# Output-weight mixing in a fused attention and maxout kernel: the same work planned at wider spacing, its stores later

## The chip, the core and the metric

The kernel runs on one NeuronCore of a Trainium2 chip. The engines are named as the profile names them: PE does the matrix products (PEld is its weight load), DVE, ACT and POOL do elementwise work, and SP issues all the DMAs of the stage that this document is about. The metric is the device time of one execution in microseconds; a smaller number is better. Before the change it is 638.62 us, the median of three runs (637.04 to 640.19).

## What is computed

Attention within chunks of 64 positions, then a layer that takes the maximum of three products, then an output layer:

```python
scores = scale * np.matmul(q_c, k_c.transpose(0, 1, 2, 4, 3))
attn = np.exp(scores - np.max(scores, axis=-1, keepdims=True))
attn = attn / (np.sum(attn, axis=-1, keepdims=True) + 1e-09)
x = np.matmul(attn, v_c)                       # as 4608 rows of 512
h = np.maximum(np.maximum(x @ w1, x @ w2), x @ w3)   # 768 columns
return h @ w_out                                     # 512 columns
```

Every fp32 operand of a large product is kept as a high and a low part, and one product is three PE instructions: low by high, high by low, high by high.

## The kernel before

The 36 tiles of 128 rows go in six pieces. Two groups of four tiles are multiplied plainly (`moe`). The other 28 tiles go in four units of 7, 8, 7 and 6 tiles (`unit`), which use a scheme with seven block products in the place of eight. The seven are taken in the order 1, 6, 5, 2, 7, 3, 4 (`ORDER`). For this scheme the weights must be mixed first: sums and differences of 256-wide blocks.

**The inner layers.** A unit runs nine "layers" (`hidden(n)`, two 128-column blocks of one of the three inner weights each). A layer is seven block products of six PE instructions, 42 in all, of 448 columns in the first unit (line 590). Its mixed weights lie in DRAM (`w0` to `w8`; rows print them as `w_1273` and so on). They come by two loads: line 515 fetches the first part, which products 1, 2 and 4 use, and line 519 the second part, for products 6, 5, 7 and 3. There are two buffers of each part (`ring`), so the load for layer n+2 is planned for the end of layer n and can only be issued when PE has finished with layer n. In the first unit `w_1273` belongs to the third layer, `w_1145` to the fourth, `w_874` to the fifth and `w_1017` to the sixth.

**What PE needs from the other engines.** The products of a layer share PSUM banks: products 2, 7 and 3 add onto the banks of 1, 6 and 5, so ACT must have copied those banks to `kept` (line 568) first. Before the first unit, the second group's output layer is multiplied (line 172 to 174, tiles `ao`, ACT copy and store at lines 329 and 330), and its last bank is wanted by the first layer's third product. Between products PE also does three short attention steps, which this document calls an attention insert: values (line 257), scores (line 222) and transpose (line 245) of the tiles of the next unit. ACT, DVE and POOL do their softmax.

**The mixing of the output weights.** `store_out(jp)` does it for three blocks, jp 0 to 2, during the first unit. Each block does on POOL two additions that put high and low part together (`f`, line 413) and four sums (`c`, line 427); on ACT the high part of the result (`sh`, line 432); on DVE the low part (`sl`, line 436); and on SP sixteen small stores to the DRAM tensor `wo`: eight "originals" of weights as they are (lines 448 and 450) and eight "mixed" ones (line 457, four of `sh` and four of `sl`). The tiles `f`, `c`, `sh` and `sl` have one buffer each, so the blocks follow one another. `wo` is first read near the end of the unit's inner layers (line 526).

**What sets the order.** The program's order on each engine is fixed when it is built. `plan(at, pe, fn)` puts a piece of work into a list by a planned time, and `passed` writes it down when the plan's clock, which advances by a nominal time per PE step, has reached it. So the numbers are no times on the chip: they only decide what stands before what on each engine. At run time every engine and the SP queue go strictly in that order, and each instruction waits for its inputs. The SP queue also counts its transfers on eight semaphores in turn, so an issue waits until the transfer eight places earlier has landed.

Of the kernel before, what the change touches and what calls it, by code (L numbers as in the profile page):

```python
# [62 lines left out]
def chunk_attn_maxout_kernel(  # L63
# [284 lines left out]
    minus, plus, most = ALU.subtract, ALU.add, ALU.max  # L348
# [56 lines left out]
    def store_out(jp):  # L405

        j, st = 2 * jp, {}

        def whole(c):
            def fn():  # L410
                if c == 0:
                    st["f"] = att.tile([P, 2, DO], F32, name="f", tag="qs", bufs=1)
                nc.gpsimd.tensor_tensor(out=st["f"][:, c], in0=woh[:, j + c].bitcast(F32), in1=wol[:, j + c].bitcast(F32),
                                        op=plus)
            return fn

        def part(k, c):
            return lambda: st["f"][:, c, k * 256:(k + 1) * 256]

        def sums(k):  # L420
            return lambda: st["c"][:, k]

        def sum_of(k, x, y, op, first=False):
            def fn():
                if first:
                    st["c"] = att.tile([P, 4, 256], F32, name="c", tag="rv", bufs=1)
                nc.gpsimd.tensor_tensor(out=st["c"][:, k], in0=x(), in1=y(), op=op)
            return fn

        def high():  # L430
            st["h"] = late["hold"].tile([P, 4, 256], F32R, name="sh", tag="k0", bufs=1)
            nc.scalar.copy(out=st["h"], in_=st["c"])

        def low():
            st["l"] = late["hold"].tile([P, 4, 256], F32R, name="sl", tag="k1", bufs=1)
            nc.vector.tensor_tensor(out=st["l"], in0=st["c"], in1=st["h"].bitcast(F32), op=minus)

        def to(first, step, many, m, h):
            w = outer_w["w"].rearrange("p (m i j h x) -> p m i j h x", m=2, i=7, j=3, h=2)
            return w[:, m, first:first + step * (many - 1) + 1:step, jp, h]  # L440

        def originals():
            if jp == 0:
                outer_w["w"] = dram.tile([P, 14 * 768], F32, name="wo")
            for h, src in enumerate((woh, wol)):
                for m in range(2):
                    cols = slice(m * P, (m + 1) * P)
                    nc.sync.dma_start(out=to(0, 3, 2, m, h), in_=src[:, j:j + 2, cols].bitcast(F32))
                    cols = slice(256 + m * P, 256 + (m + 1) * P)
                    nc.sync.dma_start(out=to(6, 1, 1, m, h), in_=src[:, j + 1:j + 2, cols].bitcast(F32))  # L450

        def mixed():
            for h, src in enumerate("hl"):
                for m in range(2):
                    cols = slice(m * P, (m + 1) * P)
                    for half in range(2):
                        nc.sync.dma_start(out=to(1 + 3 * half, 1, 2, m, h),
                                          in_=st[src][:, 2 * half:2 * half + 2, cols].bitcast(F32))

        a11, a12, a21, a22 = part(0, 0), part(0, 1), part(1, 0), part(1, 1)  # L460
        return [(0.0, whole(0)), (1.1, whole(1)), (1.5, originals), (2.2, sum_of(1, a21, a22, plus, True)),
                (2.9, sum_of(0, sums(1), a11, minus)), (3.6, sum_of(2, a11, a21, minus)),
                (4.3, sum_of(3, a12, sums(0), minus)), (5.6, high), (6.8, low), (8.4, mixed)]

    turns = [0, 0]

# [306 lines left out]
    def plan(at, pe, fn):  # L773
        heapq.heappush(due, (at, len(order), pe, fn))
        order.append(fn)
# [109 lines left out]
    def stores_out():  # L885
        for jp in range(3):
            for at, fn in store_out(jp):
                plan(now + 11.5 + 8.0 * jp + at, 0.0, fn)

    inner = 3 * JT * CT * STEP + UNITS[0] * TILE  # L890
    def span(u):
# [2 lines left out]
    def outer_span(u):  # L894
# [3 lines left out]
    parts += [("steps", lambda j=j, w=w: g["hidden"](j, w)) for j in range(JT) for w in range(3)]  # L898
    parts += [("do", change), ("do", lambda: operands(0, OPERANDS)), ("do", lambda: last_operands(0, 10.5)),
              ("do", stores_out),  # L900
              ("do", lambda: tiles(1, 4 * JT * STEP + span(0))), ("do", lambda: load(0, 0, 0.0, 1.0)), ("do", lambda: load(0, 1, 2.0, 3.0))]
    parts += [("steps", lambda: g["project"](0, 1)), ("steps", lambda: g["project"](2)), ("steps", lambda: g["project"](3))]
# [11 lines left out]
    now = -10.0  # L914
# [54 lines left out]
```

## Time and profile before

| | before |
|---|---|
| median of three runs | 638.62 us (637.04 to 640.19) |
| profiled execution, its own time | 638.54 us |
| its span, first to last instruction | 636.8 us |
| mean granted PE clock | 0.992 |
| busy share of PE / PEld / DVE / ACT / POOL | 97 / 84 / 70 / 44 / 46 % |

The profile is one execution. Times in rows are microseconds from the first instruction; the time outside the span is 1.7 us. The stage of the change lies between 175 and 235 us.

### The profile page before, as it was taken

The page shows a single profiled execution, that of the slowest core. Times are in us where ns is not written, and L with a number is a line of the kernel's source. Part 1 is how long each engine was busy: PE and PEld are TensorE (multiplying, and loading weights), DVE is VectorE, ACT ScalarE, POOL GpSimd, SP SyncE. Part 2 cuts the span into 40 slices and gives each one's busy share as a digit, 9 for nine tenths or more (in the row PEclk, how much of TensorE's full clock was granted, in tenths as well). Part 3 has the DMA queues.
Part 4 walks back from the last instruction along what each step waited for, and adds up shares of the span by engine and source line. Part 5 has one row for each costly group of instructions (what it writes and reads, how often), then busy time and mean ns, then how long its engine had stood idle before and what let it go on. Part 6 is the DMA issues. An engine that isn't in the chain of part 4 may idle for free.

```text
span 636.8 us, 12715 instructions
## 1 busy us (share of the span) xinstructions
PE 618.1 (97%) x5101; PEld 536.1 (84%) x5102; DVE 444.8 (70%) x676; ACT 277.3 (44%) x491; POOL 294.8 (46%) x243
## 2 busy tenths in 40 slices
PE   7899999999988799999999999999999999999997
PEld 3788878878877689899887888888999999999997
DVE  4889854788856566879648687895496668366761
ACT  4888633454533253535424342443342435332341
POOL 2423577765487333435524353472253437233441
PEclk9999999999989799999999999999999999999999
DMA  8978459576968976548946474578655659776675
GB/s 327 376 282 308 181 183 355 213 243 231 349 200 253 307 309 227 227 171 297 374 183 267 157 286 155 227 260 325 251 214 195 248 190 306 262 269 247 232 257 188
DMA packets 52042, 161.26 MB, mean 253 GB/s; under 512 B 5264, under 2 KB 21392, under 8 KB 46224
## 3 DMA queue, kind: packets, MB, share of 16 engines
q1 hardware_dynamic: 51984, 160.45, 70.3%
q8 instruction: 40, 0.66, 0.4%
q14 instruction: 18, 0.15, 0.1%
HBM read 128.97 MB, written 31.46 MB: 252 GB/s over the span
## 4 chain that ended last, share of the span: by engine, by line
PE 80%; DVE 9%; ACT 3%; DMA 3%; POOL 2%; issue 2%; SPq 0%; POOLq 0%; ACTq 0%; DVEq 0%
PE pm L590 61%; PE pm L172 4%; PE pm L173 4%; PE pm L174 4%; PE s L257 2%; DMA ring<-w 2%; PE tp L245 2%; PE s L222 2%; DVE e L232 1%; DVE s L383 1%; DVE sm L180 1%; DVE mx L227 1%; PE pm L735 1%; ACT e L236 1%; DMA w<-s 1%
## 5 line engine op out<-in xcount | busy, mean ns | idle before, releaser
L590 PE MATMUL pm<-X,ring 128*128 128x448 f32 (+2 forms) x1584 | 333.6, 368 | 9.5 <-DMA ring<-w 5.2
L590 PEld LDWEIGHTS pm<-X,ring 128*128 128x128 f32 x1584 | 293.0, 190 | 39.8 <-ACT kept L568 3.8
L568 ACT COPY kept<-pm 128x448 f32<-128x448 f32 (+2 forms) x132 | 69.7, 533 | 141.8 <-PE pm L590 118.1
L590 PE MATMUL pm<-Y,ring 128*128 128x448 f32 (+2 forms) x432 | 91.7, 364 | 0.0
L575 POOL TENSOR_TENSOR kept<-kept 128x448 f32<-128x448 f32 (+2 forms) x44 | 55.7, 1265 | 76.6 <-ACT kept L568 76.2
L590 PEld LDWEIGHTS pm<-Y,ring 128*128 128x128 f32 x432 | 79.4, 188 | 7.8 <-DVE Y L626 0.5
L601 DVE TENSOR_TENSOR most<-pm,most 128x448 f32<-128x448 f32 (+2 forms) x72 | 44.6, 620 | 46.3 <-PE pm L590 45.4
L172 PE MATMUL pm<-xh,wl 128*128 128x512 f32 (+1 forms) x156 | 60.8, 390 | 0.0
L173 PE MATMUL pm<-xl,wh 128*128 128x512 f32 (+1 forms) x156 | 58.4, 374 | 0.3 <-DVE xl L268 0.3
L174 PE MATMUL pm<-xh,wh 128*128 128x512 f32 (+1 forms) x156 | 58.4, 375 | 0.0
L189 POOL TENSOR_TENSOR e<-e,sm 128x512 f32<-128x512 f32 x26 | 27.9, 1074 | 62.4 <-DVE sm L186 56.7
L579 POOL TENSOR_TENSOR kept<-kept 128x448 f32<-128x448 f32 (+2 forms) x24 | 30.7, 1279 | 49.3 <-DVE kept L571 44.8
L571 DVE TENSOR_TENSOR kept<-pm,kept 128x448 f32<-128x448 f32 (+2 forms) x44 | 27.2, 618 | 35.5 <-PE pm L590 30.5
L626 DVE TENSOR_TENSOR Y<-most,Y 128x448 fp32r<-128x448 f32 (+2 forms) x60 | 48.9, 834 | 3.5 <-ACT Y L623 3.1
L623 ACT CAST Y<-most 128x448 fp32r<-128x448 f32 (+2 forms) x60 | 33.3, 568 | 24.0 <-DVE most L601 16.9
L227 DVE TENSOR_REDUCE mx<-s 128x8 f32<-128x512 f32 x36 | 24.6, 684 | 22.9 <-PE s L222 22.9
L232 DVE TENSOR_TENSOR e<-s,mx 128x512 f32<-128x512 f32 x36 | 24.8, 689 | 16.8 <-ACT stage L271 16.4
L236 ACT ACTIVATE e<-e 128x512 f32<-128x512 f32 x36 | 22.8, 632 | 30.8 <-DVE e L232 30.8
L172 PEld LDWEIGHTS pm<-xh,wl 128*128 128x128 f32 x156 | 29.4, 188 | 5.5
L174 PEld LDWEIGHTS pm<-xh,wh 128*128 128x128 f32 x156 | 29.4, 188 | 5.4
L250 ACT COPY xs<-tp 128x512 f32<-128x512 f32 x36 | 21.0, 583 | 29.7 <-PE tp L245 29.6
L173 PEld LDWEIGHTS pm<-xl,wh 128*128 128x128 f32 x156 | 29.4, 189 | 5.1 <-DVE xl L268 0.5
(98 smaller groups left out, 860.0 us busy)
## 6 DMA issues: line engine op xcount, KB each, us to landing
ring<-w SPq DMA_DIRECT2D x36, 1024.0 KB, 6.6
ring<-w SPq DMA_DIRECT2D x36, 768.0 KB, 4.5
ring<-wo SPq DMA_DIRECT2D x28, 768.0 KB, 5.4
buf<-in_qk SPq DMA_DIRECT2D x36, 512.0 KB, 6.6
buf<-in_vb SPq DMA_DIRECT2D x36, 256.0 KB, 5.9
w<-s SPq DMA_DIRECT2D x9, 1024.0 KB, 5.4
stage<-in_w SPq DMA_DIRECT2D x7, 512.0 KB, 4.9
out_t<-ao SPq DMA_DIRECT2D x16, 224.0 KB, 4.1
```

Of the source, the lines that this page charges most:

```text
L172: nc.tensor.matmul(out=o, lhsT=al, rhs=bh, start=first, stop=False)
L173: nc.tensor.matmul(out=o, lhsT=ah, rhs=bl, start=False, stop=False)
L174: nc.tensor.matmul(out=o, lhsT=ah, rhs=bh, start=False, stop=last)
L227: nc.vector.tensor_reduce(out=st["mx"].rearrange("p (g c) -> p c g", c=2), in_=st["s"], axis=AX.X, op=ALU.max)
L232: nc.vector.tensor_tensor(out=st["e"].rearrange("p g c k -> p c g k"), in0=st["s"], in1=most.unsqueeze(3).broadcast_to([P, 2, 4, 64]), op= ...
L568: return lambda: nc.scalar.copy(out=kept(k), in_=o[i])
L575: (0.95, lambda: nc.gpsimd.tensor_tensor(out=kept(2), in0=kept(2), in1=kept(0), op=plus))],
L579: (1.0, lambda: nc.gpsimd.tensor_tensor(out=c22(), in0=kept(3), in1=kept(1), op=plus))],
L590: nc.tensor.matmul(out=o[i], lhsT=a, rhs=b, start=new and k == 0, stop=last and k == 2, skip_group_check=i in banks_of_product)
L601: return lambda: nc.vector.tensor_tensor(out=M(k, c), in0=of(), in1=M(k, c), op=most)
L623: return lambda: nc.scalar.copy(out=y_room(i, jp)[:, 0, :half], in_=t[i]())
L626: return lambda: nc.vector.tensor_tensor(out=y_room(i, jp)[:, 1, :half], in0=t[i](), in1=y_room(i, jp)[:, 0, :half].bitcast(F32), op=minus)
```

## The change

Two tables of planned times change, nothing else. The steps of one block are spread from 8.4 to 17 planned us. The blocks begin at 16, 30 and 44 planned us after the output layer of the second group begins, where it was 11.5, 19.5 and 27.5. The work and the bytes are the same.

```diff
-        return [(0.0, whole(0)), (1.1, whole(1)), (1.5, originals), (2.2, sum_of(1, a21, a22, plus, True)),
-                (2.9, sum_of(0, sums(1), a11, minus)), (3.6, sum_of(2, a11, a21, minus)),
-                (4.3, sum_of(3, a12, sums(0), minus)), (5.6, high), (6.8, low), (8.4, mixed)]
+        return [(0.0, whole(0)), (2.1, whole(1)), (3.5, originals), (4.2, sum_of(1, a21, a22, plus, True)),
+                (5.9, sum_of(0, sums(1), a11, minus)), (7.6, sum_of(2, a11, a21, minus)),
+                (9.3, sum_of(3, a12, sums(0), minus)), (12.0, high), (13.4, low), (17.0, mixed)]
...
-                plan(now + 11.5 + 8.0 * jp + at, 0.0, fn)
+                plan(now + 16.0 + 14.0 * jp + at, 0.0, fn)
```

On ACT, around the end of the second group's output layer and the first layer of the unit, there stands before (`sh` is the mixing, `kept` and `most` are the layer's copies, `xs`, `stage` and `e` an attention insert's):

```order
166 L236 ACTIVATE e<-e 128x512
167 L432 CAST sh<-c 128x1024
168 L329 COPY ao<-pm 128x512
169 L568 COPY kept<-pm 128x448 x3
170 L577 COPY most<-pm 128x448
171 L432 CAST sh<-c 128x1024
172 L250 COPY xs<-tp 128x512
173 L271 COPY stage<-s 128x2x4x64
174 L236 ACTIVATE e<-e 128x512
175 L568 COPY kept<-pm 128x448 x3
176 L432 CAST sh<-c 128x1024
```

and now:

```order
166 L236 ACTIVATE e<-e 128x512
167 L329 COPY ao<-pm 128x512
168 L568 COPY kept<-pm 128x448 x3
169 L577 COPY most<-pm 128x448
170 L250 COPY xs<-tp 128x512
171 L271 COPY stage<-s 128x2x4x64
172 L236 ACTIVATE e<-e 128x512
173 L432 CAST sh<-c 128x1024
174 L568 COPY kept<-pm 128x448 x3
...
178 L568 COPY kept<-pm 128x448 x3
179 L432 CAST sh<-c 128x1024
```

The first `sh` moved from before the `ao` copy to before the second layer's `kept` copies, and the second one from the end of the first layer to the third layer.

On SP, from the second block's last originals to the loads for the fifth layer, there stands before:

```order
128 L450 DMA wo<-woh 128x128
129 L210 DMA buf<-in_qk 128x1024
130 L457 DMA wo<-sh 128x2x128 x4
131 L457 DMA wo<-sl 128x2x128 x4
132 L515 DMA ring<-w_1273 128x1536
133 L519 DMA ring<-w_1273 128x2048
...
144 L457 DMA wo<-sh 128x2x128 x4
145 L457 DMA wo<-sl 128x2x128 x4
146 L515 DMA ring<-w_1145 128x1536
147 L519 DMA ring<-w_1145 128x2048
...
150 L515 DMA ring<-w_874 128x1536
151 L519 DMA ring<-w_874 128x2048
```

and now, from the load for the third layer to the second part of that for the fifth:

```order
119 L515 DMA ring<-w_1273 128x1536
120 L519 DMA ring<-w_1273 128x2048
...
123 L457 DMA wo<-sh 128x2x128 x4
124 L457 DMA wo<-sl 128x2x128 x4
125 L448 DMA wo<-woh 128x2x128
...
132 L450 DMA wo<-wol 128x128
133 L515 DMA ring<-w_1145 128x1536
134 L519 DMA ring<-w_1145 128x2048
...
137 L515 DMA ring<-w_874 128x1536
138 L457 DMA wo<-sh 128x2x128 x4
139 L457 DMA wo<-sl 128x2x128 x4
140 L519 DMA ring<-w_874 128x2048
```

Before, all mixed stores of two blocks stood ahead of the third layer's load. Now none does; the first block's mixed stores and the second block's originals (16 issues) stand between the loads for the third and the fourth layer, and the second block's mixed stores between the two parts of the fifth layer's.

On PE the order of the instructions is the same as before.

## Rows read from the trace of the kernel before

**Rows 1.** The page: busy time by engine, and the costliest group.
```profile
PE 618.1 (97%) x5101; PEld 536.1 (84%) x5102; DVE 444.8 (70%) x676; ACT 277.3 (44%) x491; POOL 294.8 (46%) x243
...
L590 PE MATMUL pm<-X,ring 128*128 128x448 f32 (+2 forms) x1584 | 333.6, 368 | 9.5 <-DMA ring<-w 5.2
```

**Rows 2.** Timeline of PE: start, duration, line, operands, count, [idle before, releaser].
```profile
178.79 2.59 PE L590 MATMUL pm<-X,ring 128*128 128x448 f32 x12
183.72 6.74 PE L590 MATMUL pm<-X,ring 128*128 128x448 f32 x24 [2.34 <-ACT ao L329]
...
197.60 5.13 PE L590 MATMUL pm<-X,ring 128*128 128x448 f32 x24 [0.60 <-ACT kept L568]
...
205.38 1.47 PE L590 MATMUL pm<-X,ring 128*128 128x448 f32 x6 [0.97 <-DMA ring<-w]
209.82 9.74 PE L590 MATMUL pm<-X,ring 128*128 128x448 f32 x36 [2.98 <-DMA ring<-w]
220.79 1.45 PE L590 MATMUL pm<-X,ring 128*128 128x448 f32 x6 [1.23 <-DMA ring<-w]
...
228.88 6.50 PE L590 MATMUL pm<-X,ring 128*128 128x448 f32 x30 [1.25 <-ACT kept L568]
```

**Rows 3.** Chain of waits, undisturbed: attention insert, then 48 products (start, duration).
```profile
235.38 0.62 PE s L257 x32
...
237.06 9.73 PE pm L590 x48
```

**Rows 4.** Windows: length, busy us of PE, PEld, DVE, ACT, POOL; granted clock.
```profile
184.00:187.00 3.00, 3.00 (x9) 2.68 (x9) 0.73 (x3) 1.07 (x3) 2.10 (x2) 0.50 0.78 251
208.00:214.00 6.00, 4.17 (x11) 3.77 (x12) 2.19 (x5) 2.12 (x4) 0.95 (x1) 0.50 0.83 217
221.00:224.00 3.00, 3.00 (x76) 2.56 (x76) 1.62 (x3) 0.58 (x2) 1.49 (x1) 1.00 1.00 410
```

**Rows 5.** Timeline of ACT around the first and second `sh`.
```profile
182.13 1.05 ACT L432 CAST sh<-c 128x1024 fp32r<-128x1024 f32 x1 [0.15 <-POOL c L427]
183.09 0.58 ACT L329 COPY ao<-pm 128x512 f32<-128x512 f32 x1
...
192.45 1.05 ACT L432 CAST sh<-c 128x1024 fp32r<-128x1024 f32 x1 [3.90 <-POOL c L427]
...
197.03 1.38 ACT L568 COPY kept<-pm 128x448 f32<-128x448 f32 x3
```

**Rows 6.** Timeline of the SP queue: start of issue, duration, transfer.
```profile
197.63 2.40 SPq L457 DMA_DIRECT2D wo<-sl  x4
200.13 0.41 SPq L515 DMA_DIRECT2D ring<-w  x1
200.58 0.46 SPq L519 DMA_DIRECT2D ring<-w  x1
...
209.71 0.32 SPq L450 DMA_DIRECT2D wo<-wol  x1
...
215.57 0.41 SPq L515 DMA_DIRECT2D ring<-w  x1
```

**Rows 7.** Waits of the SP queue, 200 to 216: total us, times, longest.
```profile
SPq L450 <- DMA ring<-w: 4.0, 1, 4.0
```

**Rows 8.** Line 515, three loads issued 200 to 221, issue to landing.
```profile
DMA to landing us min/median/max: 5.1/5.1/7.3
```

**Rows 9.** Line 519, three loads issued 200 to 221, issue to landing.
```profile
DMA to landing us min/median/max: 7.1/9.1/10.6
```

**Rows 10.** Line 519, three loads issued 240 to 270, issue to landing.
```profile
DMA to landing us min/median/max: 6.3/6.5/6.5
```

**Rows 11.** Line 436 (`sl`): duration ns min/median/max; then timelines of DVE and POOL.
```profile
L436 DVE TENSOR_TENSOR sl<-c,sh x3: 1224/1226/2321, 183.2 to 203.8; 128x1024 fp32r<-128x1024 f32 x3
...
193.54 2.32 DVE L436 TENSOR_TENSOR sl<-c,sh 128x1024 fp32r<-128x1024 f32 x1 [1.23 <-ACT sh L432]
...
193.49 3.52 POOL L413 TENSOR_TENSOR f<-woh,wol 128x512 f32<-128x512 f32 x2
```

## Prediction

> **What bounds the kernel now.** I read the page first. PE is busy 97% of the span, and its largest group, the layers' products at line 590, has 9.5 us of idle time before it, most of it put down to DMA [rows 1]. Since PE is full elsewhere, only these idle stretches can be won back. The waits of PE by stretch put all of them into 180 to 229 us, the first four layers of the first unit; after 235 us PE waits for nothing. So whatever is won or lost here goes through to the end.
>
> PE's timeline names six stops [rows 2]: 2.34 us for the copy of `ao`, 0.60 for `kept`, 0.97 and 2.98 for the third layer's load, 1.23 for the fourth's, and 1.25 for `kept` again, 9.37 together. Two of them cost twice. Undisturbed, 48 products take 9.73 us, 0.203 each, and an attention insert 1.68 (235.38 to 237.06) [rows 3]. After the 2.34 stop 24 products take 6.74 instead of 4.87, and after the 2.98 stop 36 take 9.74 instead of 7.30: 1.8 and 2.4 us lost. The granted clock was 0.50 in these stretches, the lower of the two levels, and 1.00 after the 1.23 stop [rows 4]. Each stop also has a tail: 24 products at full clock after the 0.60 stop take 5.13, 0.25 above 4.87.
>
> The causes stand on ACT and SP. The mixing's first `sh` waited 0.15 us for POOL and ran 1.05 ahead of the `ao` copy [rows 5]. On SP the third layer's load was issued at 200.13, right after the second block's `sl` stores [rows 6]. PE had finished the first layer, and with it the buffer, near 193.3 (24 products to 190.4, an insert, six more) [rows 2, 3]. The load was 6.8 us late. The fourth layer's load, at 215.57, came right behind the third block's stores, 12.9 us after its buffer was free at 202.7 (197.60 + 5.13) [rows 2].
>
> **The change, part by part.** POOL, ACT, DVE and SP do the same instructions; only places move. I lay the new order along PE, with 1.22 us for six products and 1.68 for an insert.
>
> (a) *The `ao` copy.* Without `sh` ahead it starts 1.05 + 0.15 = 1.2 us earlier, and PE goes on at 182.5 after a stop of about 1.15. The nearest row is the 1.23 stop, after which the clock stayed at 1.00 [rows 2, 4], so the 1.8 us go too: gain 3.0. If the clock falls all the same, it is 1.2.
>
> (b) *`kept` in the second layer.* The 0.60 stop came when the second `sh` and the doubled `sl` (2.32) pushed the insert's work on ACT, and `kept` with it, to 197.03 [rows 5, 11]. Neither stands there now: gain 0.85 with its tail. But the first `sh` now stands right ahead of these copies, and the second right behind those of the third layer. POOL's fourth sum for the first `sh` follows an addition that waits for product 7 of the first layer (18 products after 182.5, 186.2); by an estimate it is done before 191, so `sh` runs 191 to 192 and the first `kept` is there by 192.5; product 2 needs it at 194. It costs nothing while that cover of 1.5 us holds; bounds are 0 and 0.6 a place by the row of before. I take 0.3 at each: -0.6.
>
> (c) *The third layer's load.* From 182.5: 24 products to 187.4, an insert to 189.1, six to 190.3. Now the load is issued there, at 190.4 and 190.9, with 16 transfers fewer ahead. It lands 6.5 (undisturbed) to 10.6 us after issue [rows 9, 10], 197.4 to 201.5; its second part is needed at 201.7 (18 + 24 products to 198.8, insert to 200.5, six more). So both stops go: 0.97 + 2.98 + 2.4 for the clock + 0.5 for two tails = 6.85.
>
> (d) *The fourth layer's load.* It has the first block's 8 mixed stores and the second block's 8 originals ahead of it. An issue waits for the transfer eight places earlier: before, line 450 waited 4.0 us for a load in this way, till 209.71 [rows 6, 7]. So the second `sl` store cannot go before the third layer's load has landed, near 198. Then 3 stores and 8 originals of some 0.52 us (2.40 for four with small waits [rows 6]) make 5.7, and the load is issued at 203.7 and 204.2; its buffer was free at 198.8, so it is still 5 us late. The third layer ends 42 products after 200.5, at 209.0; its first part lands 5.1 later at 208.8 [rows 8]. The second is needed six products and an insert on, at 211.9. By the landings 7.1 and 9.1 it comes at 211.3 to 213.3; the mean, 212.3, is 0.4 late. Bounds: on time, or with everything at 9.1 (landing third layer 200.0, issue 206.3) at 215.4, 3.5 late. The stop of 1.23 + 0.25 shrinks to 0.4: gain 1.1.
>
> (e) *`kept` in the fourth layer*, 1.25: the same ACT and DVE order, PE going on with it, so it stays [rows 2]. DVE has the second block's `sl` (1.22) a little earlier, in the third layer, which pushes the chain by 0 to 1.2; there is idle time on DVE ahead of the copies, so nearer 0: -0.2.
>
> (f) *The fifth layer's load.* This is new. Its first part is issued when the third layer ends, 209.1, but the second stands behind 8 mixed stores, and the eighth of these waits for the landing of the first part, 5.1 to 7.3 us on [rows 8]. I take 6.1, as two loads and the fourth layer's are nearly drained by then: 215.2, the second part goes at 215.7. With 6.5 (little is queued ahead) it lands at 222.2. PE needs it at: 211.9 + 0.4, 18 products, the stop (e), 18 more (220.7 without the 0.4), six of the fifth layer: 222.3. No slack: I take 0.3 for a stop, between 0 and 5.2 (7.3 and then 10.6: 227.5).
>
> (g) *The rest.* The third block's originals and mixed stores now go out until about 233, one layer ahead of what overwrites `woh` and `wol` (near 242) and 40 us ahead of the first read of `wo`. The sixth layer's load, behind eight originals whose last waits for the fifth's second part, goes at 224.5 and is needed at 231 to 234. I cost these at nothing; the cover is 3 to 10 us.
>
> **Sum**: 3.0 + 0.85 - 0.6 + 6.85 + 1.1 - 0.2 - 0.3 = 10.7. From the profiled 638.54 (span 636.8 and 1.7 outside) that gives **627.8**; the median of the runs, 638.62, is the same within 0.1.
>
> **The rivals.**
>
> *1. The loads stay late.* The moved stores now stand ahead of other loads. For it: in (d) 16 issues are still ahead, in (f) there is no slack. Against: the stores' stretch now has 14 planned us a block. With the second part of the fifth layer issued at 216.9 and 10.6 on the way, PE stops 5.2 us, with 2.4 for the clock and a tail 7.85: 635.3. With the fourth's at 215.4 instead it is 3.5 + 2.65, 633.5; the two don't add, since the later PE is, the less the other is late. The Trainium skill (DMA: Bandwidth & Descriptors, Queues, rings and completion order) says that each DMA engine takes the descriptors of a queue in order, so that a load drains behind the stores issued ahead of it; by that rule this rival is the case. The rows agree in part: 9.1 and 10.6 beside stores against 6.5 [rows 9, 10].
>
> *2. POOL gets in DVE's way.* `sl` took 2.32 beside POOL's `f` and 1.22 without [rows 11]. If the spread-out `f` (1.76 each) meets the short chain on DVE ahead of `kept` in (e), the stop grows by 1.3 to 2.5, where the clock fell: +3.7, 631.5. Against: by my layout `f` ends at 211.4 and the chain begins near 213.5. The Trainium skill (SBUF — State Buffer, Who interferes with whom) has the rule: a DVE instruction with two SBUF inputs and a POOL instruction that reads SBUF share a port, and the later blocks. The 2.32 agrees with it.
>
> *3. It does not do what it says at the first stop*: PE's wait for `ao` is really one for something else that came last. Then (a) is nothing: 630.8. Against: `ao` ends and PE starts within 0.1 us [rows 2, 5].
>
> *4. Slower.* The fifth layer's load waits twice in the queue: its first part takes 10.6 (landing 219.7, which holds the eighth store), its second part, issued at 220.2, 10.6 again: 230.8, 8.5 late, with clock and tail 11.15, which gives 638.7. It decides from a landing past 231 on; every us later is a us slower than before. For it: the waiting rule of [rows 7] is certain. Against: no first part took more than 7.3 here.
>
> **How the numbers follow.** Forecast (626 to 630) 0.62; rival 1 0.15; rival 2 0.10; rival 3 0.08; rival 4 0.05. A measurement of this kernel can tell about 0.5%, 3.2 us, so faster means below 635.4: all of the first, half of rival 1 and rivals 2 and 3, 0.87. Within 0.5%: the other half of rival 1 and half of rival 4, 0.10; slower 0.03. The range goes down to 626.0 (no costs in b, d, e and f and a little of the `ao` stop) and up to rival 1 at 635.4.
>
> **What would show it.** PE's timeline after: a stop of about 1.2 near 181.4 with the clock at 1.00 after it; none at the third layer; 0 to 0.5 in the fourth ahead of product 6; 1.3 for `kept`; at most 0.5 ahead of product 6 of the fifth. On SP the third layer's load near 190.4, the fourth's near 203.7, the two parts of the fifth's some 6.6 us apart. It is wrong if the granted clock shows 0.50 anywhere past 182, or if PE names `ring` for more than 2 us.

## The result, and the profile after

The changed kernel takes 632.76 us, the median of eight runs (630.71 to 635.71); the kernel before took 638.5 in eight runs on the same chip. The ratio is 0.9916 with a 95% interval of 0.989 to 0.9941: faster by 5.7 us, where 10.7 was forecast. The time lies inside the range (626.0 to 635.4), well above the 627.8 that the sum gave. Single runs of the changed kernel scatter over 5 us, those of before over 3. The profiled execution of after took 635.71 (span 633.9), the longest of its eight, and is only 2.8 under the profiled execution of before; a second profile of the same kernel, below, took 634.37.

PE's timeline after, its stops alone (columns as in [rows 2]):

```profile
181.89 5.13 PE L590 MATMUL pm<-X,ring 128*128 128x448 f32 x24 [0.91 <-ACT ao L329]
203.98 5.23 PE L590 MATMUL pm<-X,ring 128*128 128x448 f32 x24 [0.23 <-ACT kept L568]
212.24 1.45 PE L590 MATMUL pm<-X,ring 128*128 128x448 f32 x6 [3.04 <-DMA ring<-w]
220.34 5.28 PE L590 MATMUL pm<-X,ring 128*128 128x448 f32 x24 [1.31 <-ACT kept L568]
226.49 1.45 PE L590 MATMUL pm<-X,ring 128*128 128x448 f32 x6 [0.87 <-DMA ring<-w]
237.73 2.71 PE L590 MATMUL pm<-X,ring 128*128 128x448 f32 x12 [0.68 <-DMA ring<-w]
249.19 3.33 PE L590 MATMUL pm<-X,ring 128*128 128x448 f32 x15 [0.99 <-DMA ring<-w]
549.99 58.51 PE L590 MATMUL pm<-X,ring 128*128 128x384 f32 x336 [1.98 <-DMA ring<-w]
```

Of the six stops of [rows 2], both for the third layer's load are gone, and after the stop for `ao` 24 products take 5.13 and not 6.74. The stop for the fourth layer's load has grown from 1.23 to 3.04, and there are new ones at the fifth, sixth and seventh layer, which the sum had at 0.3, 0 and 0.

How far PE is ahead of the kernel before, at the same place of its order (differences of the starts in both timelines of PE):

| place | before | after | ahead by | since the row above | forecast |
|---|---|---|---|---|---|
| start of the first layer | 178.79 | 178.38 | 0.41 | | |
| insert in the first layer | 190.38 | 186.95 | 3.43 | +3.0 | (a) +3.0 |
| insert behind the second layer | 202.66 | 198.35 | 4.31 | +0.9 | (b) +0.85 - 0.3 |
| end of the third layer | 219.56 | 209.21 | 10.35 | +6.0 | (c) +6.85 - 0.3 |
| insert in the fourth layer | 222.17 | 213.62 | 8.55 | -1.8 | (d) +1.1 |
| insert in the fifth layer | 235.31 | 227.87 | 7.44 | -1.1 | (e), (f) -0.5 |
| insert in the sixth layer | 246.72 | 240.37 | 6.35 | -1.1 | (g) 0 |
| insert in the seventh layer | 257.52 | 252.46 | 5.06 | -1.3 | (g) 0 |
| end of the span | 636.8 | 633.9 | 2.9 | -2.2 | 0 |

So PE was 10 us ahead at the end of the third layer, as forecast, and gave half of it back within the next four, for loads that came late.

The SP queue after shows why (columns as in [rows 6]):

```profile
192.43 3.35 SPq L457 DMA_DIRECT2D wo<-sh  x4
195.87 5.08 SPq L457 DMA_DIRECT2D wo<-sl  x4
201.00 1.48 SPq L448 DMA_DIRECT2D wo<-woh  x1
...
206.42 0.37 SPq L515 DMA_DIRECT2D ring<-w  x1
...
209.24 0.33 SPq L515 DMA_DIRECT2D ring<-w  x1
209.66 2.83 SPq L457 DMA_DIRECT2D wo<-sh  x4
214.62 5.32 SPq L457 DMA_DIRECT2D wo<-sl  x4
219.99 0.68 SPq L519 DMA_DIRECT2D ring<-w  x1
```

The waits of that queue from 186 to 250 (total, times, longest) name what it waited for:

```profile
SPq L457 <- DMA ring<-w: 9.9, 5, 2.7
...
SPq L450 <- DMA ring<-w: 1.6, 1, 1.6
SPq L457 <- DMA buf<-in_qk: 1.3, 2, 0.9
```

The fourth layer's load goes at 206.4 (203.7 in the forecast). Of these 2.7 us, 1.4 are lost by the first original, at 201.0: the four `sl` stores waited 1.6 us for the third layer's load and then 0.3 and 0.9 for the two input loads behind it. The rest is lost in the eight originals, which take 5.4 us and not 4.2; the first issue alone took 1.48, and the profile names no wait for it.

The second part of the fifth's load goes at 220.0 (215.7 in the forecast). The last `sl` store ahead of it waited 2.7 us, till 219.58, for the landing of the load's own first part. From issue (209.24) to landing that part took:

```profile
DMA to landing us min/median/max: 10.3/10.3/10.3
```

At nearly the same moment, 219.95, landed the store that stands eight places ahead of the second part. The chain of waits (start, duration) goes by that store:

```profile
209.66 10.29 DMA wo<-sh
...
219.99 6.37 DMA ring<-w
...
228.18 9.41 DMA ring<-w
```

That store of 128 KB was issued behind the fourth layer's load, two input loads and the first part of the fifth's. From issue to landing, the four `sh` stores of the second block, issued 209.7 to 212.1 after the change; and those issued 195.3 to 197.0 before it:

```profile
DMA to landing us min/median/max: 9.0/10.1/10.3
```

```profile
DMA to landing us min/median/max: 4.2/4.4/4.7
```

### The profile page after: what moved, and what is told of

The parts are those of the page before. It is cut to its first block, busy times and chain, and to the rows that moved or that the text cites. A ratio compares the mean times of both kernels' runs of the same rounds, so it can differ in the third digit from the quotient of the medians.

```text
span 633.9 us, 12714 instructions
## 1 busy us (share of the span) xinstructions
PE 614.7 (97%) x5101; PEld 532.6 (84%) x5102; DVE 446.6 (70%) x676; ACT 277.1 (44%) x491; POOL 295.1 (47%) x243
## 4 chain that ended last, share of the span: by engine, by line
PE 73%; DVE 12%; DMA 8%; ACT 4%; issue 2%; POOL 1%; SPq 0%; POOLq 0%; ACTq 0%; DVEq 0%
PE pm L590 55%; DMA ring<-w 5%; PE pm L172 4%; PE pm L173 4%; PE pm L174 4%; PE s L257 2%; DVE X L501 2%; PE tp L245 2%; PE s L222 2%; DMA wo<-sh 2%; DVE e L232 1%; DVE s L383 1%; DVE mx L227 1%; DVE sm L180 1%; ACT e L236 1%
## 5 line engine op out<-in xcount | busy, mean ns | idle before, releaser
L590 PE MATMUL pm<-X,ring 128*128 128x448 f32 (+2 forms) x1584 | 330.8, 365 | 10.1 <-DMA ring<-w 7.6
L590 PEld LDWEIGHTS pm<-X,ring 128*128 128x128 f32 x1584 | 289.6, 188 | 40.8 <-ACT kept L568 3.5
L189 POOL TENSOR_TENSOR e<-e,sm 128x512 f32<-128x512 f32 x26 | 28.1, 1081 | 67.3 <-DVE sm L186 50.7
L571 DVE TENSOR_TENSOR pm<-pm,kept 128x448 f32<-128x448 f32 (+2 forms) x48 | 30.1, 627 | 5.2 <-PE pm L590 4.2
```

The costliest lines, as they stand in the source:

```text
L571: return lambda: nc.vector.tensor_tensor(out=out(), in0=o[i], in1=kept(k), op=plus)
L590: nc.tensor.matmul(out=o[i], lhsT=a, rhs=b, start=new and k == 0, stop=last and k == 2, skip_group_check=i in banks_of_product)
```

## The experiments

Three theories stood against one another. **Q**: a layer's load is late because of what stands ahead of it on SP. **B**: the bytes slow the landings wherever they stand. **P**: the gain came from spreading POOL's work. An edit is given against the changed kernel unless it says otherwise, and medians are given beside that of the kernel before in the same runs.

### The two halves of the change

The blocks apart, but each with its tight steps of before:

```diff
-        return [(0.0, whole(0)), (2.1, whole(1)), (3.5, originals), (4.2, sum_of(1, a21, a22, plus, True)),
+        return [(0.0, whole(0)), (1.1, whole(1)), (1.5, originals), (2.2, sum_of(1, a21, a22, plus, True)),
...
-                (9.3, sum_of(3, a12, sums(0), minus)), (12.0, high), (13.4, low), (17.0, mixed)]
+                (4.3, sum_of(3, a12, sums(0), minus)), (5.6, high), (6.8, low), (8.4, mixed)]
```

> One half of the change alone: the blocks begin where the changed kernel begins them, but each block keeps the tight steps of before, so POOL works in the same bunches as before and the stores of a block come sooner. Theory Q: the first stop is as in the changed kernel (0.9) and the third layer's load goes near 191.5 behind the first block's mixed stores, so both early stops are gone; the fourth layer's load has its second part behind eight mixed stores and stops PE by 1 to 4 us; median 630 to 635. Theory P: the gain of the spreading is gone, median 636 to 638.5.

Measured: 633.99 against 639.3, ratio 0.9917 (0.9889 to 0.9945), the same gain as the whole change. Four of its stops on PE:

```profile
181.49 3.91 PE L590 MATMUL pm<-X,ring 128*128 128x448 f32 x18 [0.88 <-ACT ao L329]
...
206.07 6.34 PE L590 MATMUL pm<-X,ring 128*128 128x448 f32 x30 [1.40 <-ACT kept L568]
...
216.32 9.20 PE L590 MATMUL pm<-X,ring 128*128 128x448 f32 x36 [2.22 <-DMA ring<-w]
...
229.85 2.30 PE L590 MATMUL pm<-X,ring 128*128 128x448 f32 x6 [2.27 <-DMA ring<-w]
```

The third layer's load goes at 191.5, and no stop for it is left. The second part of the fourth's goes at 210.3, behind eight mixed stores, and stops PE 2.22 us with slow products behind it; both came as Q said. P is out: with POOL in its old bunches the gain is there. The bunches have stops of their own (1.40 for `kept` in the third layer, where the changed kernel has 0.23), but in the time the spreading within a block added nothing that these runs can tell.

The first step alone, on the kernel before: only the first block's high and low part come behind the copy of `ao`; the mixed stores keep their planned time.

```diff
-                (4.3, sum_of(3, a12, sums(0), minus)), (5.6, high), (6.8, low), (8.4, mixed)]
+                (4.3, sum_of(3, a12, sums(0), minus)), ((8.0, 5.6, 5.6)[jp], high), ((8.1, 6.8, 6.8)[jp], low), (8.4, mixed)]
```

> The kernel before with one step moved: only the first block's high and low part and with them its mixed stores come some 2 planned us later, so that the first sh stands behind the copy of ao. Theory Q: the 2.34 us stop shrinks to about 1 and the clock after it stays at 1.00, which gives 1.2 + 1.8 = 3.0 us; the later stops at the third and fourth layer's loads are as before or a little longer, since those loads stand behind the same stores, so half or more of it may be given back: median 635.5 to 637.5. Theory P: no change, 638.5.

Measured: 639.41 against 639.3, ratio 1.0004 (0.9985 to 1.0023).

```profile
181.85 5.13 PE L590 MATMUL pm<-X,ring 128*128 128x448 f32 x24 [1.03 <-ACT ao L329]
196.33 6.75 PE L590 MATMUL pm<-X,ring 128*128 128x448 f32 x24 [2.81 <-ACT kept L568]
207.16 7.54 PE L590 MATMUL pm<-X,ring 128*128 128x448 f32 x36 [1.19 <-DVE most L601]
218.62 2.58 PE L590 MATMUL pm<-X,ring 128*128 128x448 f32 x6 [3.92 <-DMA ring<-w]
```

The first stop fell to 1.03 and its 24 products to 5.13: term (a) is there, 3 us. None of it reaches the end. The second block's `sh` is still in its old place, and the `kept` copies behind it, at 195.76 (197.03 before, [rows 5]), now stop PE 2.81 us with slow products after them (6.75): at the next insert PE is 0.3 us behind the kernel before (203.00 and 202.66). The third layer's load, at 198.37, does not stop PE any more, so that PE is 4.9 us ahead at the end of that layer (214.70 and 219.56). But the fourth layer's load, at 213.66, then stops it 3.92 us where it was 1.23, with the clock at 0.50 after it, and the lead is gone. Q had "half or more given back"; it was all of it.

### Stores moved from ahead of the loads to behind them

The second block's originals behind the fourth layer's load:

```diff
-        return [(0.0, whole(0)), (2.1, whole(1)), (3.5, originals), (4.2, sum_of(1, a21, a22, plus, True)),
+        return [(0.0, whole(0)), (2.1, whole(1)), ((3.5, 9.5, 3.5)[jp], originals), (4.2, sum_of(1, a21, a22, plus, True)),
```

> The changed kernel with one group moved: the second block's eight originals come right behind the load for the fourth layer, not right ahead of it. Theory Q (the queue: a layer's load is late because of the issues that stand ahead of it on SP): the fourth layer's load goes at about 201, not 206.4, the 3.0 us stop at the fourth layer is gone or under 0.5, and the median falls by about 3, to 629.5; what follows (0.9, 0.7, 1.0 us at the next three layers) stays. Theory B (bytes: the stores slow the landings wherever they stand): the load goes earlier but takes longer than 6 us to land, the stop stays above 1.5 us, median 631 to 633. Theory P (what the change gave comes from POOL's work being spread, the queue matters little): no change, 632.8.

Measured: 632.5 against 639.3, ratio 0.99 (0.9861 to 0.9938). And all groups of the second and third block, each behind a load:

```diff
-                (9.3, sum_of(3, a12, sums(0), minus)), (12.0, high), (13.4, low), (17.0, mixed)]
+                (9.3, sum_of(3, a12, sums(0), minus)), (12.0, high), (13.4, low), ((17.0, 18.0, 24.0)[jp], mixed)]
```

with the originals at `(3.5, 9.5, 14.0)[jp]`.

> The changed kernel with the stores of the second and third block moved so that each group of eight stands behind a layer's load and none right ahead of one or inside one: originals of block two behind the fourth layer's load, mixed of block two behind the fifth's, originals of block three behind the sixth's, mixed of block three behind the seventh's. Theory Q: the stops of 3.0, 0.9, 0.7 and 1.0 us at the fourth to seventh layer go with their tails of 0.25, in all 6.6, and the median falls to about 626. Theory B: at most half of it, 629 to 631. Theory P: no change, 632.8.

Measured: 631.59 against 639.3, ratio 0.988 (0.9847 to 0.9913). Q had 629.5 and 626 for the two, so it missed both times, and neither can be told from the changed kernel by its time. The order did what Q said: in the first of the two the fourth layer's load went at 201.6, in the second at 200.2, and in neither does PE stop for it; the second has a stop of 1.07 left, at the eighth layer's load. That the first median lies in B's range is not for B's reason: the two parts of that load took 4.7 and 8.8 us to land in the first kernel, 5.6 and 9.3 in the second (5.7 and 7.7 in the changed kernel), and both were in time. Where PE had stopped for the load, it now stops a little later for `kept`: 3.34 us in the first kernel, with 8.42 for the 30 products after it, and in the second

```profile
218.59 8.12 PE L590 MATMUL pm<-X,ring 128*128 128x448 f32 x30 [3.31 <-ACT kept L568]
```

That is 2.0 us more than the 1.31 in the changed kernel, and the 30 products take 8.12 where after the 1.25 of [rows 2] they took 6.50. This stop is a second limit, which lay hidden under the first. The chain of waits of the second kernel leads back from it along DVE (start, duration):

```profile
205.67 1.62 DVE sl L436
...
207.75 1.18 DVE Y L626
...
209.51 2.15 DVE most L601 x2
...
218.10 0.44 ACT kept L568
```

In the third layer stands the second block's `sl`, and of the layer's own steps two are longer than their 0.62: the low part `Y` with 1.18 and the second of the two maximum steps with 1.61. POOL ran the third block's `f` beside them (timelines of DVE and POOL):

```profile
210.05 1.61 DVE L601 TENSOR_TENSOR most<-kept,most 128x448 f32<-128x448 f32 x1
...
206.17 2.28 POOL L413 TENSOR_TENSOR f<-woh,wol 128x512 f32<-128x512 f32 x1
...
209.90 1.26 POOL L413 TENSOR_TENSOR f<-woh,wol 128x512 f32<-128x512 f32 x1
```

### The chain on DVE

Theory D is that POOL's `f` and the `sl` lengthen this chain. Its rival S is that the stop is what is left when PE runs early. The kernel with all stores moved is the base. First, the third block's `f` and what follows it moved out of the third layer (`whole` at `(0.0, 0.0, 8.0)[jp]` and `(2.1, 2.1, 10.1)[jp]`, the rest of that block after them):

> The kernel with the stores moved behind the loads, and besides only the third block's two additions f, with the sums and sh and sl behind them, moved out of the third layer on POOL. Theory D (the 3.3 us stop for kept in the fourth layer comes from the chain of DVE in the third, which is lengthened by POOL's f beside it and by the second block's sl in it): the 1.18 us low part and the 1.57 to 1.61 us maximum on DVE fall to 0.62 each, the stop falls by about 1.5 to 1.8 us, the clock after it stays at 1.00 (2 us more), median 628 to 630 against 631.6. Rival S (the stop is due to PE running earlier against a fixed chain on ACT): the stop stays at 3.0 to 3.3.

Measured: 629.72 against 639.1, ratio 0.9857 (0.9827 to 0.9886). `Y` and the maximum are at 0.61 each:

```profile
207.37 0.61 DVE L626 TENSOR_TENSOR Y<-most,Y 128x448 fp32r<-128x448 f32 x1
...
209.09 0.61 DVE L601 TENSOR_TENSOR most<-kept,most 128x448 f32<-128x448 f32 x1
```

Then instead the second block's `sh` and `sl` moved to the fifth layer (`((12.0, 27.5, 23.5)[jp], high), ((13.4, 28.1, 24.5)[jp], low)`, its mixed stores and the third block's sums after them; the third block's originals come earlier again, at 4.0):

> The kernel with the stores moved behind the loads, and besides only the second block's sh and sl (and what must follow them) moved out of the third layer into the fifth; POOL's f stays beside DVE's chain in the third layer. Theory D: the chain loses sl's 1.62 us, the stop for kept falls from 3.3 to about 1.7, the clock stays at 1.00, median 627.5 to 630. Rival S: the stop stays at 3.0 to 3.3 and the median at 631 to 632.

Measured: 630.32 against 639.1, ratio 0.9857 (0.9834 to 0.9879). Then both, with the third block's `f` later still (14.8):

> Both moves together: neither f nor sh and sl stand in the third layer, and each group of eight stores has a layer's load of its own to follow. Theory D: the stop for kept is that of the kernel before or less, 0.5 to 1.3 us, no load stops PE for more than 1 us, the granted clock shows 1.00 throughout, median 625 to 627.5. Rival S: 631 to 632.

Measured: 629.08 against 639.1, ratio 0.9862 (0.9825 to 0.9899). PE's stops for `kept` in the fourth layer, of the three in this order:

```profile
216.51 6.50 PE L590 MATMUL pm<-X,ring 128*128 128x448 f32 x30 [1.64 <-ACT kept L568]
```

```profile
217.74 6.59 PE L590 MATMUL pm<-X,ring 128*128 128x448 f32 x30 [2.22 <-ACT kept L568]
```

```profile
217.34 6.51 PE L590 MATMUL pm<-X,ring 128*128 128x448 f32 x30 [1.31 <-ACT kept L568]
```

From 3.31 to 1.64 without `f`, to 2.22 without `sl` (1.7 was expected), to 1.31 without both, and the 30 products are back at 6.5 to 6.6. D holds for this stop, S does not. The time follows less fully: the last kernel is 629.1 where 625 to 627.5 was expected, and the second, 630.3, lies just above its range. Other stops stand in its place: 1.21 for `kept` in the fifth layer of the first, 1.47 for the sixth layer's load and 1.68 for DVE at the seventh in the second; in the last, 0.64 and 0.42 for the loads of the sixth and seventh layer and 1.24 for `ao`. By their time the three can't be told from one another, and their intervals meet that of the kernel with all stores moved; all three medians lie under the 632.0 of the changed kernel in the same runs (below).

The counter-test leaves the stores where the changed kernel has them, and moves only the third block's POOL, ACT and DVE steps out of the third layer; its mixed stores follow them:

> The changed kernel with its stores where they are, and only the third block's POOL, ACT and DVE steps out of the third layer. Theory H (two limits side by side: in the changed kernel the late load of the fourth layer hides the lengthened chain of DVE): the maximum on DVE beside f falls from 1.57 to 0.62 but PE's stops stay at 2.3 to 3.0 for the load and 1.3 for kept, median 631.5 to 633. Rival: the time falls by 1.5 to 2 as it did when the stores had been moved, to 630 to 630.5.

Measured: 631.89 against 638.54, ratio 0.9902 (0.9885 to 0.9919). The maximum is at 0.61, and PE stops all the same, 2.12 us at the fourth layer's load and 1.31 for `kept`:

```profile
210.80 1.46 PE L590 MATMUL pm<-X,ring 128*128 128x448 f32 x6 [2.12 <-DMA ring<-w]
...
218.90 5.28 PE L590 MATMUL pm<-X,ring 128*128 128x448 f32 x24 [1.31 <-ACT kept L568]
```

So there are two limits side by side: to shorten one of them alone changes nothing that the time shows.

### The fifth layer's load, and a second look at the changed kernel

The second block's mixed stores behind both parts of the fifth layer's load, and nothing else:

```diff
-                (9.3, sum_of(3, a12, sums(0), minus)), (12.0, high), (13.4, low), (17.0, mixed)]
+                (9.3, sum_of(3, a12, sums(0), minus)), (12.0, high), (13.4, low), ((17.0, 17.4, 17.0)[jp], mixed)]
```

> The changed kernel with one group moved: the second block's eight mixed stores come behind the second part of the fifth layer's load, not between its two parts. Theory Q: that part is issued near 209.6 and not 220 (or 222, second profile), so its stop of 0.9 to 1.2 us at the fifth layer goes; the stop of 2.3 to 3.0 at the fourth layer stays as it is; median lower by about 1, 631. Theory B: the part lands no sooner than 8 us later because of the bytes ahead, but 8 us is still in time, so the same; the stops of the sixth and seventh layer may grow by up to 1 as the originals and mixed stores now go out closer together.

Measured: 633.84 against 638.54, ratio 0.992 (0.9898 to 0.9943), no gain. The fifth layer's stop is gone, as said, and the fourth's is 1.74, less than the 2.3 to 3.0 that should have stayed. But the sixth layer's load stops PE 2.0 us longer, not "up to 1". It went out behind sixteen stores in a row, at 226.0, 2.2 us sooner than in the changed kernel, and took 10.5 us to land (9.4), so that it came 1.0 sooner, while PE came 3.0 sooner. The clock fell after that stop (0.54 from 236.7 to 239.5), and what was left went with it:

```profile
236.69 4.23 PE L590 MATMUL pm<-X,ring 128*128 128x448 f32 x12 [2.67 <-DMA ring<-w]
```

The changed kernel once more:

> The changed kernel once more, for a second profile beside the others of this chip. Theory V (part of the profiled time, the 1.98 us stop at 550 in the last unit, is a landing that varies from run to run and has nothing to do with the change): the stops up to 250 come again within 0.3 us each, the one at 550 does not or has another size; median 631 to 634. Rival: the change moves the last unit's loads for good, and the stop at 550 comes again with about 2 us.

Measured: 632.04 against 639.1, ratio 0.9894 (0.9873 to 0.9916). Its profile:

```profile
213.40 1.46 PE L590 MATMUL pm<-X,ring 128*128 128x448 f32 x6 [2.34 <-DMA ring<-w]
...
228.01 1.45 PE L590 MATMUL pm<-X,ring 128*128 128x448 f32 x6 [1.23 <-DMA ring<-w]
```

The stops of the loads come again, each with another size (2.34 and 1.23 for 3.04 and 0.87; 0.91 and 0.39 at the next two). They are less steady than the 0.3 expected, and the loads' landings set them: the fourth layer's load went 8.0 us after the end of the second layer (8.1 in the first profile) and its first part took 5.0 us to land, not 5.7. The stop at 550 does not come again: there the load landed in 6.7 us after its issue, where it took 9.2 in the first profile. So it is a landing that varies, as V said, and no lasting work of the change.

## Why the prediction was right in direction and half in size

**What bounds the kernel** was right: all that was won stands in the first layers, and nothing after 260 us differs but one landing that varies. The time lies in the range, but not in the band of 626 to 630 that had 0.62; it lies where the prices of rivals 1 to 3 lay (630.8 to 635.3), so that the range was wide enough is in part luck. Of the prediction's own two signs of being wrong one came: PE names `ring` for more than 2 us (3.04, and 2.34 in the second profile). The other did not: the granted clock shows 1.00 from 182 to 262 in both profiles.

**(a)** 3.0 forecast, 3.0 found: a stop of 0.91, and no slow products after it. Rival 3 is out. **(b)** 0.85 forecast, 0.9 found. The 0.3 taken twice for `sh` beside the copies was not needed: the second layer has no stop, and the 0.23 in the third comes before the second `sh` runs (204.67) and is there without it (0.22 in the kernel with `sh` and `sl` moved to the fifth layer). **(c)** 6.0 found, 6.85 less 0.3 forecast; the load went at 189.9 and was in time.

**(d) is the step that failed**: +1.1 forecast, -1.8 found. The rule that an issue waits for the landing of the transfer eight places earlier was used, but only for the third layer's load, and the rest of the stores were priced at 0.52 each. The landings of the two input loads that stood between count too (0.3 and 0.9 of waiting), the third layer's load landed at 198.6 and not 198, and the originals took 5.4 us and not 4.2. So the load went 2.7 us later than in the sum. The stop is also another than the one that was priced: the sum had the first part in time, at 208.8, and the second 0.4 late ahead of product 6. The stop stands ahead of product 1, for the first part, which landed at 212.1, and behind it the second part was in time. Bounds of 0 and 3.5 had been named; it came out at 3.04 and 2.34, and 0.4 was taken, near the wrong end.

**(f)** had the right path and a wrong size: the last store did wait for the landing of the load's first part, but that took 10.3 us, where 6.1 was taken because little else would be left in the queue. 0.87 and 1.23 found, 0.3 forecast; it was no more because (d) had made PE late (the second part was needed at 225.6 and not 222.3). **(e)** held at 1.31 in the changed kernel, but for a reason that the sum didn't have: the late load before it gave the longer chain on DVE the time it needed. Rival 2 was present all along and cost nothing only because rival 1 stood ahead of it; the experiments with moved stores took that cover away and show the stop 2.0 us longer, with slow products besides, and 1.7 us of it go with `f`. The rule of SBUF — State Buffer, Who interferes with whom in the Trainium skill, cited with rival 2, agrees with the low part at 1.18 and the maximum at 1.57 to 1.61 beside `f` and 0.61 without it.

**(g)** "cost at nothing" failed: 0.68 and 0.99 at the sixth and seventh layer (0.91 and 0.39 the second time). The sum had the sixth layer's load go at 224.5; it went at 227.75, some 3.5 us after PE had left its buffer (the fourth layer ends 18 products after 220.34), since the last original waited till 226.38 for the fifth's second part and two input loads stood next. The seventh's, at 239.08, was about as late, behind a mixed store that waited 2.7 us for the sixth's second part. The second parts then landed after 9.4 and 9.5 us, with the third block's stores queued around them; [rows 10] has 6.5 for a load without them. Which of the two lengths decides, the late issue or the slow landing, no run separates.

**The rivals.** Rival 1 is the nearest to what happened, though with four stops in the place of one: 635.7 and 634.4 in the two profiled executions, 632 to 633 in the medians; the price of 635.3 was for one stop with a slow clock, and no clock fell. By the rule of the Trainium skill cited there (DMA: Bandwidth & Descriptors, Queues, rings and completion order), a DMA engine takes a queue's descriptors in order, so that a load drains behind the stores ahead of it. The rows show it the other way round as well: the stores behind the loads landed after 9.0 to 10.3 us, where they had taken 4.2 to 4.7 before. The first half of rival 4 came as written: its first part of the fifth's load took 10.6 and the second went at 220.2, and they were 10.3 and 219.99. The line against it, that no first part took more than 7.3, did not hold. Its second half did not come: the second part landed after 6.4 us, not 10.6.

Of 10.7 us forecast, (d) took 2.9, (e) and (f) 0.6, (g) 2.4 and the landing at 550 us 2.2 in the profiled execution; the last did not come in the second profile. In the experiments, with the stores behind the loads and `f` out of the third layer, the medians are 9.4 and 10.0 us under the kernel before.

## What to carry to other kernels

Where each transfer's issue waits for the landing of one some places earlier, price a store in a busy queue by the landings that it waits for and its own landing behind the loads, not by its issue alone, and give each group of stores a load to follow rather than one to precede. When one wait is removed, lay out the next chain beside it with the new neighbours on the other engines: here two limits of about 3 us covered each other, and each alone, taken away, brought nothing that the runs can tell. A term that is measured right at its place (3.0 us at the first stop) is a gain only if nothing behind it takes it back, and in one kernel here all of it was taken.

## What was not expected of the hardware

**Small stores behind loads.** 128 KB took 1.9 to 3.3 us to land in the changed kernel with little ahead (originals, 201 to 206 us) and 9.0 to 10.3 when 3.3 MB of loads had been issued in the 3.3 us before (the fourth layer's parts of 768 and 1024 KB, two inputs of 256 and 512, the first part of the fifth's).

**The clock and the length of a stop.** The granted clock fell after stops of 2.34, 2.98 [rows 4] and 3.31, but not after the 3.04 of the changed kernel, nor after the 2.34 of its second profile (1.00 from 213.4 to 217.0). Windows (columns as in [rows 4]), first of the changed kernel after its stop, then of the kernel with all stores moved:

```profile
212.30:216.00 3.70, 3.70 (x78) 3.23 (x79) 2.10 (x4) 1.12 (x3) 3.01 (x3) 1.00 1.02 394
```

```profile
218.60:222.00 3.40, 3.40 (x12) 2.87 (x13) 3.37 (x6) 2.30 (x5) 3.39 (x4) 0.70 1.06 350
```

PE had been busy since 203.98 without a stop before the first of them (5.23 us of products), and for an insert and 18 products before the second, after an equally busy layer. What decides between them stays open: no run tries it. It means that the 1.8 and 2.4 us of the sum for the clock were right at their places, but not a rule for stops of that length.
